# Eight token groups instead of seven, and one more sequence in head-by-head layout, in a retention and snake-FFN kernel

## The chip, the cores and the metric

The kernel runs on one core of a Trainium2 chip. The metric is the device time of one execution in microseconds (us). One core has five engines that run at the same time, each with its own instruction stream in a fixed order: TensorE (PE, matrix multiplies; its weight loads are listed as PEld), VectorE (DVE), ScalarE (ACT), GpSimd (POOL) and SyncE (SP, which here only starts transfers). Transfers (DMAs) are started from SP, ACT or POOL and run beside the engines. Matrix products land in PSUM, eight banks of 2 KB on each of 128 partitions; everything else is kept in SBUF.

## What is computed

The first part is a retention layer with a state of its own for each batch entry and head, the second a feed-forward layer with a snake activation:

```python
batch, n_heads, seq, head_dim = (4, 8, 768, 64)
gamma = 1.0 - 2.0 ** (-5.0 - np.arange(H))
for t in range(S):
    state = gamma[None, :, None, None] * state + einsum('bhd,bhe->bhde', k[:, :, t], v[:, :, t])
    y[:, :, t] = scale * einsum('bhd,bhde->bhe', q[:, :, t], state)
# y as [3072 tokens, 512]
h = x @ w_in            # 512 -> 2048
s = np.sin(alpha * h)
g = h + s * s / (alpha + 1e-09)
out = g @ w_out         # 2048 -> 512
```

## The kernel before

**Chunks and sequences.** A sequence is one batch entry: 768 tokens, cut into six chunks of 128. There are 24 chunks. The list `order` (called `P` further down) puts the four first chunks of the four sequences at the front (`e0` to `e3`, `P[0]` to `P[3]`), then the other five of each sequence: `P[4..8]` are of sequence 0, `P[9..13]` of sequence 1, `P[14..18]` of sequence 2 and `P[19..23]` of sequence 3.

**Groups and phases.** The feed-forward layer works on groups of chunks, `sizes` of them (L49). `phase(g, ...)` (L543) walks over the 16 blocks of the hidden dimension of group g. One step of it (a slot) takes one block of 128 hidden units for a group of four chunks (512 columns), or two blocks for a group of two chunks (twice 256 columns). In a slot come the first product `ph` (L425), the sine on ScalarE (L428), the square (L433, or L435 on VectorE for a few slots), a piece of attention if the table `att` has one for this slot, the sum into `gT` on VectorE (L440), and some of the second product `po` (L450) of the group before, spread evenly over the slots. A finished `po` tile is copied by ScalarE (L462) and stored by SP (L463). Group 0 and the start are written out by hand.

**Attention of a chunk.** Within a chunk, attention is a masked product of q and k, plus a product of q with the state that the sequence has so far. It has two forms. In the narrow form q, k and v of a chunk lie as 128 tokens by 8 heads: `stage_A` makes the scores (L265), VectorE masks them (L269, 128x1024), `stage_M` multiplies with the state (L299) and with v (L303), makes the new state (`stage_S`, L279), scales the result into `xT` (L310), and ScalarE copies the state (`keep_S`, L286). In the wide form (`wide(j)`, L86) the partitions hold 64 tokens twice, the lower half for heads 0 to 3 and the upper half for heads 4 to 7, so that TensorE can work as four tiles of 64x64: `scores` (L337, L341), the mask (L346, 128x768), and `burst`, which does `inter` of the old chunk (L327), `scores` of the next, and `mix` of the old one (L354, L357, L366). What `burst` leaves behind is handed to the next slot: `exit` (two VectorE products into `xT`, L377), `keep` (two VectorE sums into the float32 state `s_f`, L384 or L386) and `hand` (two copies of `s_f` into the bf16 state `s_bd`, L391, by ScalarE or GpSimd). The next `inter` of the same sequence reads `s_bd`.

**Loads.** GpSimd starts all loads of q, k and v, because they turn float32 into bf16 on the way. `load_chunk` (L83) brings one chunk of one tensor in one transfer, 128 KB in bf16. `load_seq` (L103) brings the wide chunks of a whole sequence, one tensor at a time, in eight transfers, one for each head, and is in the order q, k, v. v has to be scaled by a decay before it is used (`scale_v`, L137), for nearly all chunks on GpSimd and in the same instruction stream as the loads. That stream is written out by hand from L670 to L694; an instruction in it that waits holds up all behind it.

**Turned copies.** `turn(j)` (L256) starts a DMA on SP that writes the transposed q and k of one chunk to `qkT`; it needs all of q and k of this chunk, which for a wide chunk means all eight transfers of each. It is placed two chunks ahead: the slot that makes the scores of `P[n]` starts the turn of `P[n+2]`. SP's queue holds these turns and the stores, in order.

**Slots.** `where[n]` is the (phase, slot) at which the scores of `P[n]` and the rest of the attention of `P[n-1]` stand. Before, `where` is (1,1), (1,3), (1,6) for n = 6 to 8, then slots 0, 2, 4, 6 of phase 2 for `P[9]` to `P[12]`, and slots 2, 6, 10, 14 of phases 3 to 5. Phase g makes the attention of group g + 1. Below, (2,1) stands for slot 1 of phase 2.

Of the kernel before, what the change touches and what calls it, by code (L numbers as in the profile page):

```python
# [9 lines left out]
BF16 = mybir.dt.bfloat16  # L10
# [5 lines left out]
def kernel(  # L16
# [15 lines left out]
    nc = tc.nc  # L32
    B, H, S, D = q.shape
    C = 128
    NCH = S // C
    NJ = B * NCH
# [9 lines left out]

    order = [b * NCH for b in range(B)]
    order += [b * NCH + c for b in range(B) for c in range(1, NCH)]
    sizes = [4, 2, 2, 4, 4, 4, 4]  # L49
    assert sum(sizes) == NJ  # L50
    NG = len(sizes)
    groups = [order[sum(sizes[:g]):sum(sizes[:g + 1])] for g in range(NG)]
# [14 lines left out]
    raw = {}  # L67
# [5 lines left out]
    def load_chunk(j, names="qkv"):  # L73
        for name, src in (("q", q), ("k", k), ("v", v)):
            if name not in names:
                continue
            if name == "v":
                t = big.tile([128, H, D], BF16, name="vr", tag="vr", bufs=NJ - 9)
            else:
                if ("qk", j) not in raw:  # L80
                    raw["qk", j] = big.tile([128, 2, H, D], BF16, name="qkr", tag="qkr", bufs=NJ - 10)
                t = raw["qk", j][:, "qk".index(name)]
            nc.gpsimd.dma_start(out=t, in_=chunk_of(src, j))  # L83
            raw[name, j] = t

    def wide(j):  # L86
        return j >= 2 * NCH + 2 and j != 3 * NCH

    def load_seq(bt, names="qkv"):

# [42 lines left out]
    def scale_v(j, eng):  # L133
        t, by = raw["v", j], kg
        if wide(j):
            t, by = t.rearrange("i f p d -> i (f p) d"), kgq
        eng.tensor_mul(t, t, by[:, j % NCH, :, None].to_broadcast([128, H, D]))  # L137
# [150 lines left out]
    def stage_M(j):  # L288
        c = j % NCH
        g, i = place[j]  # L290
        if g not in xT:
            xT[g] = work.tile([128, KS, sizes[g] * C], BF16, name="xT", tag="xT", bufs=3)
        qkT, aT, vs = st["qkT", j], st["aT", j], raw["v", j]
        py = psum.tile([128, NP, 128], F32, name="py", tag="ty")
        if c > 0:
            for p in range(NP):
                for e in range(2):
                    r = slice(64 * e, 64 * e + 64)
                    nc.tensor.matmul(py[r, p, :], s_bd[c % 2][:, p, r], qkT[:, p, :],  # L299
                                     start=(p == 0), stop=True, skip_group_check=True)  # L300
        for p in range(NP):
            for e in range(2):
                nc.tensor.matmul(py[64 * e:64 * e + 64, p, :], vs[:, 2 * p + e, :], aT[:, e, p, :],  # L303
                                 start=(c == 0 and p == 0), stop=True, skip_group_check=True)
        x = xT[g][:, :, i * C:(i + 1) * C]
        if c == 0:
            nc.scalar.copy(x, py)
            return
        ps = stage_S(j) if c < NCH - 1 else None
        nc.vector.tensor_mul(x, py, qg[:, c])  # L310
        if ps is not None:
            keep_S(j, ps)
# [36 lines left out]
    def mix(j, first=None):  # L349

        py, aT, vs, c = st["py", j], st["aT", j], raw["v", j], j % NCH
        for m in range(2):
            for b, e in tiles4:
                nc.tensor.matmul(py[b][half(e), m * 128:(m + 1) * 128], vs[half(b), 0, 2 * m + e, :],  # L354
                                 aT[half(b), e, m, 0:128], start=False, stop=True, skip_group_check=True)
            for b, e in tiles4:
                nc.tensor.matmul(py[b][half(e), m * 128 + 64:(m + 1) * 128], vs[half(b), 1, 2 * m + e, :],  # L357
                                 aT[half(b), e, m, 128:192], start=False, stop=True, skip_group_check=True)
        now = j if c < NCH - 1 else first
        if now is not None:  # L360
            ks, vs = raw["k", now], raw["v", now]
            for f in range(2 if wide(now) else 1):
                for m in range(2):
                    for b, e in tiles4:
                        h = 4 * b + 2 * m + e
                        nc.tensor.matmul(py[b][half(e), 256 + 64 * m:320 + 64 * m],  # L366
                                         ks[half(b), f, 2 * m + e, :] if wide(now) else ks[:, h, :],
                                         vs[half(b), f, 2 * m + e, :] if wide(now) else vs[:, h, :],
                                         start=False, stop=True, skip_group_check=True)
        g, i = place[j]  # L370
        if g not in xT:
            xT[g] = work.tile([128, KS, sizes[g] * C], BF16, name="xT", tag="xT", bufs=3)
        x = xT[g][:, :, i * C:(i + 1) * C]

        def leave():
            for b in range(2):
                nc.vector.tensor_mul(x[:, 2 * b:2 * b + 2, :], py[b][:, 0:256].rearrange("p (m t) -> p m t", m=2),  # L377
                                     qg[:, c, 2 * b:2 * b + 2])

        def keep():  # L380
            for b in range(2):
                o, new = s_f[:, 2 * b:2 * b + 2], py[b][:, 256:384].rearrange("p (m d) -> p m d", m=2)
                if wide(now):
                    nc.vector.tensor_add(o, o, new)  # L384
                else:
                    nc.vector.tensor_copy(o, new)  # L386

        def hand():
            for e in range(2):
                copy = nc.scalar.copy if now // NCH == 2 else nc.gpsimd.tensor_copy  # L390
                copy(s_bd[(now % NCH + 1) % 2][half(e), :, half(e)], s_f[half(e)])  # L391

        more = {"exit": leave}
        if now is not None:
            more.update(keep=keep, hand=hand)
        return more
# [6 lines left out]
    def run(more, *kinds):  # L403
        for kind in kinds:
            if more and kind in more:
                more.pop(kind)()
# [136 lines left out]
    def phase(g, outs, att, nf=1, on_vector=()):  # L543


        no, done = len(outs), 0
        for n in range(FF // nf):
            more, fresh = rest[0], {}
            now = Slot(g, n * nf, nf=nf).sq("D" if n in on_vector else "A")
            run(more, "keep", "exit", "hand")  # L550
            for fn in att.get(n, ()):
                fresh.update(fn() or {})
            run(fresh, "mask")
            if fresh:
                rest[0] = fresh
            now.add()
            while done < no * (n + 1) * nf // FF:
                outs[done]()
                done += 1
# [13 lines left out]
    def SK(j):  # L573
        return lambda: keep_S(j, stage_S(j))
# [3 lines left out]
    P = order  # L578
# [91 lines left out]
    load_chunk(P[7])  # L670
    load_chunk(P[8])
    scale_v(P[6], nc.gpsimd)
    load_chunk(P[9])
    scale_v(P[7], nc.gpsimd)
    scale_v(P[8], nc.gpsimd)
    scale_v(e1, nc.gpsimd)
    load_chunk(P[10])
    for n in range(11, 15):
        scale_v(P[n - 2], nc.gpsimd)
        load_chunk(P[n])  # L680
    load_seq(2, "q")
    scale_v(P[13], nc.gpsimd)
    scale_v(e2, nc.gpsimd)
    load_seq(2, "k")
    scale_v(P[14], nc.gpsimd)
    load_seq(2, "v")
    scale_v(e3, nc.gpsimd)
    load_seq(3, "q")
    scale_v(P[15], nc.gpsimd)
    scale_v(P[16], nc.gpsimd)  # L690
    load_seq(3, "k")
    scale_v(P[17], nc.gpsimd)
    scale_v(P[18], nc.gpsimd)
    load_seq(3, "v")  # L694

    fill(1)
# [5 lines left out]
    fill(4)  # L702
    stage_M(P[5])
    fill(4)
    where = {6: (1, 1), 7: (1, 3), 8: (1, 6)}
    for g in range(2, NG - 1):
        first = P.index(groups[g + 1][0])
        for i, n in enumerate((0, 2, 4, 6) if sizes[g] == 2 else (2, 6, 10, 14)):
            where[first + i + 1] = (g, n)
    atts = {g: {} for g in range(1, NG)}  # L710

    def at(place, fn):
        atts[place[0]].setdefault(place[1], []).append(fn)

    def M_last(j):

        stage_M(j)
        nc.vector.tensor_copy(s_f, st["ps"])

    def B(old, new, first):  # L720
# [3 lines left out]
    for n in range(6, NJ + 1):  # L724
        new = P[n] if n < NJ else None
        first = new - 1 if n < NJ and new % NCH == 1 else None
        if n > 6 and wide(P[n - 1]):
            at(where[n], B(P[n - 1], new, first))
        else:
            at(where[n], lambda j=new: (scores if wide(j) else stage_A)(j))  # L730
            if n > 6:
                at(where[n], lambda j=P[n - 1], last=wide(new): (M_last if last else stage_M)(j))
            if first is not None:
                at(where[n], SK(first))
        if n + 2 < NJ:
            at(where[n], X(P[n + 2]))
        if n >= 19 and n < NJ:
            at(where[n], lambda j=new: scale_v(j, nc.gpsimd))
# [35 lines left out]
```

## Time and profile before

| what | us |
|---|---|
| three runs | 215.71, 215.79, 216.97 |
| median | 215.79 |
| the profiled execution, its own time | 216.11 |
| its span, first to last instruction | 214.3 |
| VectorE busy | 133.9 (62%) |
| ScalarE busy | 157.3 (73%) |
| GpSimd busy | 103.7 (48%) |
| TensorE's granted clock, mean | 1.000 |

The profiled execution stands 1.8 us above its span and 0.32 us above the median. TensorE is busy nearly all the time; the transfers are dense up to about 128 us and thin after that, since all of q, k and v has been loaded by then. A busy TensorE is not TensorE at its peak: the 128x512 products of L425 and L450 are shown with 379 and 380 ns each, but in a row of them they follow each other every 0.216 us (four in 0.86 us).

| line, operation | shape | count | mean ns |
|---|---|---|---|
| L428 ACT sine | 128x512 | 72 | 686 |
| L428 ACT sine | 128x256 | 32 | 470 |
| L433 ACT square | 128x512 | 82 | 630 |
| L440 DVE into gT | 128x512 | 72 | 746 |
| L440 DVE into gT | 128x256 | 32 | 476 |
| L269 DVE narrow mask | 128x1024 | 11 | 1218 |
| L346 DVE wide mask | 128x768 | 9 | 954 |
| L310 DVE narrow xT | 128x512 | 11 | 684 |
| L377 DVE wide xT | 128x256 | 18 | 416 |
| L391 ACT hand | 64x256 | 6 | 394 |

### The profile page before, as it was taken

Reading aid. Unit: us, or ns where it says so; the run is one execution under the profiler, and the core shown is the slowest. Engines: PE = TensorE matmul, PEld = TensorE weight load, DVE = VectorE, ACT = ScalarE, POOL = GpSimd, SP = SyncE. Lnnn points to the kernel's source line nnn. Section 1 sums busy time; section 2 is a strip of 40 time slices with the busy share of each in tenths; the row PEclk is TensorE's granted clock in tenths of the full one; section 3 lists DMA queues with packets and bytes.
Section 4 is the critical chain, followed back from the end, with each engine's and each line's share of the span. In section 5 each row is a group of like instructions: output and inputs, shape, how many; then the busy total and the mean of one; then the engine's idle time right before and its main releaser. Section 6 shows DMA issues by size and latency. Waiting matters only on the chain.

```text
span 214.3 us, 4656 instructions
## 1 busy us (share of the span) xinstructions
PE 201.1 (94%) x1822; PEld 108.7 (51%) x1849; DVE 133.9 (62%) x253; ACT 157.3 (73%) x299; POOL 103.7 (48%) x136
## 2 busy tenths in 40 slices
PE   7798999899999999997999999999999999999994
PEld 2444554467767664534454554554554444444453
DVE  5887859857997766866946746665765544444000
ACT  7779696757897779787697796677677778887121
POOL 8974433999397697999999213203301000000000
PEclk9999999999999999999999999999999999999999
DMA  9999999999999999999999982141011011100212
GB/s 134 146 191 185 206 207 171 154 133 240 144 159 157 136 189 155 131 97 193 161 158 115 158 133 66 35 98 54 3 50 49 3 49 49 49 38 14 98 49 98
DMA packets 101189, 24.95 MB, mean 116 GB/s; under 512 B 93728, under 2 KB 98224, under 8 KB 101168
## 3 DMA queue, kind: packets, MB, share of 16 engines
q0 software_dynamic: 77360, 13.38, 86.3%
q1 hardware_dynamic: 23664, 11.22, 26.5%
q8 instruction: 14, 0.23, 0.5%
q10 hardware_dynamic: 144, 0.07, 0.1%
q14 instruction: 7, 0.06, 0.1%
HBM read 27.27 MB, written 6.29 MB: 157 GB/s over the span
## 4 chain that ended last, share of the span: by engine, by line
PE 79%; DVE 8%; ACT 6%; DMA 3%; issue 3%; DVEq 0%; ACTq 0%
PE po L450 33%; PE ph L425 32%; ACT s L428 3%; DMA qkT<-qk_seq 3%; DVE gT L440 3%; PE spare L492 3%; ACT s L433 2%; DVE aT L269 2%; PE pa L265 2%; PE poh L473 2%; PE py L299 2%; PE py L303 1%; PE pa L337 1%; PE py L327 1%; PE ps L279 1%
## 5 line engine op out<-in xcount | busy, mean ns | idle before, releaser
L440 DVE SCALAR_TENSOR_TENSOR gT<-s,rec_alpha,ph 128x512 bf16<-128x512 f32 (+3 forms) x120 | 74.2, 638 | 55.1 <-ACT s L433 54.6
L425 PE MATMUL ph<-xT,w_in 128*128 128x512 bf16 (+3 forms) x478 | 97.9, 337 | 1.1 <-DVE xT L377 0.3
L450 PE MATMUL po<-w_out,gT 128*128 128x512 bf16 x344 | 90.8, 380 | 3.5 <-issue 2.8
L428 ACT ACTIVATE s<-ph,alpha_sb 128x512 f32<-128x512 f32 (+3 forms) x120 | 69.5, 600 | 32.9 <-PE ph L425 32.6
L425 PEld LDWEIGHTS <-w_in 128*128 128x128 bf16 x480 | 45.5, 98 | 43.0 <-issue 2.5
L433 ACT ACTIVATE s<-s 128x512 f32<-128x512 f32 (+1 forms) x90 | 55.8, 621 | 2.5
L450 PEld LDWEIGHTS <-gT 128*128 128x128 bf16 x368 | 34.0, 98 | 37.0 <-issue 0.6
L462 ACT COPY o_sb<-po 128x512 f32<-128x512 f32 x23 | 13.1, 575 | 8.5 <-PE po L450 8.4
L391 POOL CAST s_bd<-s_f 64x256 bf16<-64x256 f32 x10 | 3.9, 394 | 26.3 <-DVE s_f L384 23.2
L137 POOL TENSOR_TENSOR vr<-vr,kg 128x512 bf16<-128x512 bf16 x12 | 13.0, 1097 | 7.3 <-DMA vr<-in_v_dram 7.3
L83 POOL DMA_DIRECT2D vr<-in_v_dram x15 | 13.7, 916 | 3.5 <-DMA w_in<-in_moe_w_in_dram 1.7
L83 POOL DMA_DIRECT2D qkr<-in_q_dram x14 | 12.9, 918 | 3.6 <-DMA w_in<-in_moe_w_in_dram 1.7
L83 POOL DMA_DIRECT2D qkr<-in_k_dram x14 | 12.6, 897 | 4.0 <-DMA w_out<-in_moe_w_out_dram 3.3
L269 DVE TENSOR_TENSOR aT<-pa,mask 128x1024 bf16<-128x1024 f32 x11 | 13.4, 1218 | 0.5 <-PE pa L265 0.5
L137 POOL TENSOR_TENSOR v_seq<-v_seq,kgq 128x512 bf16<-128x512 bf16 x9 | 9.3, 1055 | 7.7 <-DMA v_seq<-in_v_dram 7.3
L103 POOL DMA_DIRECT2D qk_seq<-in_q_dram x16 | 11.3, 750 | 1.8 <-DMA vr<-in_v_dram 1.2
L103 POOL DMA_DIRECT2D qk_seq<-in_k_dram x16 | 11.2, 729 | 0.3 <-DMA qk_seq<-in_q_dram 0.3
L103 POOL DMA_DIRECT2D v_seq<-in_v_dram x16 | 11.3, 758 | 0.0
L286 ACT CAST s_bd<-ps 64x256 bf16<-64x256 f32 x24 | 8.7, 360 | 3.0 <-PE ps L279 2.7
L492 PE MATMUL spare<-warm 128*128 128x512 bf16 x27 | 8.9, 450 | 1.3 <-DVE warm L156 1.2
L310 DVE TENSOR_TENSOR xT<-py,qg 128x512 bf16<-128x512 f32 x11 | 7.5, 684 | 2.3 <-PE py L303 2.3
L346 DVE TENSOR_TENSOR aTw<-pa,maskq 128x768 bf16<-128x768 f32 x9 | 8.6, 954 | 0.5
(92 smaller groups left out, 143.9 us busy)
## 6 DMA issues: line engine op xcount, KB each, us to landing
out_dram<-o_sb SPq DMA_DIRECT2D x23, 256.0 KB, 2.3
w_in<-in_moe_w_in_dram POOLq DMA_DIRECT2D x4, 512.0 KB, 11.0
w_out<-in_moe_w_out_dram POOLq DMA_DIRECT2D x4, 512.0 KB, 14.8
vr<-in_v_dram POOLq DMA_DIRECT2D x15, 128.0 KB, 6.7
qkr<-in_q_dram POOLq DMA_DIRECT2D x14, 128.0 KB, 6.8
qkr<-in_k_dram POOLq DMA_DIRECT2D x14, 128.0 KB, 6.5
qk_seq<-in_q_dram POOLq DMA_DIRECT2D x8, 80.0 KB, 7.5
qk_seq<-in_k_dram POOLq DMA_DIRECT2D x8, 80.0 KB, 4.4
```

Source lines behind the costliest of these rows:

```text
L83: nc.gpsimd.dma_start(out=t, in_=chunk_of(src, j))
L103: nc.gpsimd.dma_start(out=o, in_=src[bt, h, cs[0] * C:, :].rearrange("(f i) d -> i f d", i=64))
L137: eng.tensor_mul(t, t, by[:, j % NCH, :, None].to_broadcast([128, H, D]))
L269: nc.vector.tensor_mul(aT.rearrange("p e n t -> p (e n) t"), pa.rearrange("p e n t -> p (e n) t"), m)
L286: nc.scalar.copy(s_bd[(j % NCH + 1) % 2][r, :, r], ps[r, :, :])
L425: nc.tensor.matmul(self.ph[:, m, :], w_in[:, i, f * 128:(f + 1) * 128], xT[g][:, i, self.lo:self.hi], start=(m == 0 and i == 0), stop=(i = ...
L428: nc.scalar.activation(out=self.s[:, m, :], in_=self.ph[:, m, :], func=ACTF.Sin, scale=alpha_sb[:, f:f + 1])
L433: nc.scalar.activation(out=self.s, in_=self.s, func=ACTF.Square)
L440: nc.vector.scalar_tensor_tensor(gT[self.g][:, f, self.lo:self.hi], self.s[:, m, :], rec_alpha[:, f:f + 1], self.ph[:, m, :], op0=ALU.mult ...
L450: nc.tensor.matmul(po[g, ts], gT[g][:, f, ts * C:(ts + 1) * C], w_out[:, f, :], start=(f == 0), stop=(f == FF - 1))
L462: nc.scalar.copy(o_sb, po[g, ts])
L492: nc.tensor.matmul(spare["ps"], warm[:, :128], warm, start=True, stop=True)
```

## The change

Groups become 4, 2, 2, 2, 2, 4, 4, 4. All chunks of sequences 1, 2 and 3 but their first ones become wide, so that six more chunks (`P[9]` to `P[14]`) are. Sequence 1 is loaded by `load_seq` in place of fifteen `load_chunk` transfers, and the eight transfers for each tensor of sequence 2 bring ten blocks of 64 tokens instead of eight. The scaling of v moves along. The order in a slot becomes `exit`, `keep`, `hand`; `hand` is ScalarE's for sequences 1 and 2. The step from narrow to wide, with its copy into `s_f`, now falls between sequences 0 and 1, at `where[9]`. Before, the table of the groups of two had slots 0, 2, 4, 6; now a group of two that is followed by another has slots 1 and 5.

```diff
-    sizes = [4, 2, 2, 4, 4, 4, 4]
+    sizes = [4, 2, 2, 2, 2, 4, 4, 4]
...
     def wide(j):
-        return j >= 2 * NCH + 2 and j != 3 * NCH
+        return j >= NCH and j % NCH > 0
...
-                copy = nc.scalar.copy if now // NCH == 2 else nc.gpsimd.tensor_copy
+                copy = nc.gpsimd.tensor_copy if now // NCH == 3 else nc.scalar.copy
...
-            run(more, "keep", "exit", "hand")
+            run(more, "exit", "keep", "hand")
...
     load_chunk(P[7])
     load_chunk(P[8])
     scale_v(P[6], nc.gpsimd)
-    load_chunk(P[9])
+    load_seq(1, "q")
     scale_v(P[7], nc.gpsimd)
+    load_seq(1, "k")
     scale_v(P[8], nc.gpsimd)
     scale_v(e1, nc.gpsimd)
-    load_chunk(P[10])
-    for n in range(11, 15):
-        scale_v(P[n - 2], nc.gpsimd)
-        load_chunk(P[n])
+    load_seq(1, "v")
+    scale_v(e2, nc.gpsimd)
     load_seq(2, "q")
-    scale_v(P[13], nc.gpsimd)
-    scale_v(e2, nc.gpsimd)
+    for j in P[9:12]:
+        scale_v(j, nc.gpsimd)
     load_seq(2, "k")
-    scale_v(P[14], nc.gpsimd)
+    for j in P[12:14]:
+        scale_v(j, nc.gpsimd)
     load_seq(2, "v")
...
-    where = {6: (1, 1), 7: (1, 3), 8: (1, 6)}
+    where = {6: (1, 1), 7: (1, 3), 8: (1, 5)}
     for g in range(2, NG - 1):
         first = P.index(groups[g + 1][0])
-        for i, n in enumerate((0, 2, 4, 6) if sizes[g] == 2 else (2, 6, 10, 14)):
+        slots = (2, 6, 10, 14) if sizes[g] == 4 else (0, 2, 4, 6) if sizes[g + 1] == 4 else (1, 5)
+        for i, n in enumerate(slots):
             where[first + i + 1] = (g, n)
...
-    def M_last(j):
-
-        stage_M(j)
+    def into_sum():
         nc.vector.tensor_copy(s_f, st["ps"])
...
-                at(where[n], lambda j=P[n - 1], last=wide(new): (M_last if last else stage_M)(j))
+                at(where[n], lambda j=P[n - 1]: stage_M(j))
             if first is not None:
                 at(where[n], SK(first))
+                at(where[n], into_sum)
```

With this, `where` is (1,5) for `P[8]`, (2,1) and (2,5) for `P[9]` and `P[10]`, (3,1) and (3,5) for `P[11]` and `P[12]`, (4,0), (4,2), (4,4), (4,6) for `P[13]` to `P[16]`, and slots 2, 6, 10, 14 of phases 5 and 6 for the rest.

## The prediction

> **What bounds the kernel now.** I read the page first, then the chain of waits in order of time, then busy time by stage, then GpSimd's timeline and the transfers' times to landing.
>
> ```profile
> span 214.3 us, 4656 instructions
> PE 201.1 (94%) x1822; PEld 108.7 (51%) x1849; DVE 133.9 (62%) x253; ACT 157.3 (73%) x299; POOL 103.7 (48%) x136
> PE 79%; DVE 8%; ACT 6%; DMA 3%; issue 3%; DVEq 0%; ACTq 0%
> ```
>
> TensorE carries the chain; one transfer holds 3% of it. The stages are phases 1 to 4, their borders the first `ph` product of each (columns: length, then busy time and instructions of each engine, clock, DMA share, GB/s).
>
> ```profile
> 47.50:61.50 14.00, 13.27 (x158) 10.00 (x160) 11.68 (x21) 11.44 (x27) 10.66 (x12) 1.00 2.07 176
> 61.50:79.96 18.46, 18.00 (x220) 12.57 (x224) 14.27 (x26) 14.94 (x35) 14.87 (x19) 1.00 1.92 163
> 79.96:107.11 27.15, 25.07 (x250) 12.61 (x252) 20.00 (x31) 22.17 (x39) 25.38 (x35) 1.00 1.75 148
> 107.11:138.57 31.46, 30.82 (x325) 15.71 (x329) 19.67 (x37) 24.67 (x42) 15.22 (x22) 1.00 1.14 113
> ```
>
> Phases 2 and 4 are full; phase 3 has 2.1 us of idle TensorE, and GpSimd works 25.38 of its 27.15. The chain says what the largest wait is, and GpSimd's timeline why:
>
> ```profile
> 91.72 5.83 DMA qkT<-qk_seq
> 97.55 0.04 issue
> 97.59 0.25 PE pa L337 x4
> ...
> 106.33 0.40 DVE s_f L384 x2
> 106.73 0.35 DVE xT L377
> 107.07 0.04 issue
> 107.11 1.02 PE ph L425 x4
> ```
>
> ```profile
> 84.19 5.48 POOL L103 DMA_DIRECT2D qk_seq<-in_k_dram  x8
> 89.60 1.13 POOL L137 TENSOR_TENSOR vr<-vr,kg 128x512 bf16<-128x512 bf16 x1
> 90.59 5.50 POOL L103 DMA_DIRECT2D v_seq<-in_v_dram  x8
> ...
> 113.39 5.75 POOL L103 DMA_DIRECT2D v_seq<-in_v_dram  x8
> ```
>
> GpSimd ends the issue of sequence 2's k at 89.67, the last of it lands at 91.5, only then can the first wide chunk be turned, and TensorE waits until 97.59. A sequence loaded head by head is late as a whole. After phase 4 the kernel does nothing but multiply.
>
> **What goes.** An attention piece on TensorE is priced by cadence. Four slots of phase 4 take 7.84 us (`po` after one burst at 112.57, after the next at 120.41), of which 4 x 1.726 = 6.90 are feed-forward: 0.94 a wide chunk. Two slots of phase 2 take 4.60 (narrow scores start at 62.47 and 67.07, at 71.78 and 76.38), of which 3.45 are feed-forward: 1.15 a narrow one. Six chunks turn wide: -1.2 us. Feed-forward itself does not change: eight products of 256 columns take 0.87, four of 512 take 0.86, and the `po` work over the phases is the same. Phase 3 is 16 x 1.294 = 20.7 plus attention of about 4.4 = 25.1, so it loses 2.0; its parts are the turn (1.1), `xT` late at the next border (0.4, mended by `exit` first) and ScalarE's lag. These 2.0 go from here. In phase 1 `stage_M(P[7])` comes a slot earlier, so the 0.26 that phase 2's first product waits for L310 goes.
>
> **What comes: ScalarE and VectorE.** Phase 5 now is the group of four after a group of two. A slot there is 1.29 on TensorE against 0.69 + 0.63 = 1.32 on ScalarE; I put 0.4 of phase 3's loss back (0 to 0.8). Phase 4 is eight slots of twice 256 columns with a burst in every second. ScalarE needs 8 x (0.84 + 0.63) + 4 x 0.80 + 2 x 0.57 = 16.1 us of some 17.6, VectorE per two slots 2 x 0.87 + 0.95 + 0.75 + 0.48 = 3.9 of 4.4: both fit, but the hand-over is tight. From the end of a slot's `ph`, the mask runs to 1.8, the sums into `gT` to 2.7, `exit` to 3.4, `keep` to 3.9, ScalarE's two copies to 4.7; the next `inter` is due at 0.94 + 0.86 + 0.87 + 0.86 + 0.87 = 4.4. That is 0.35 late, three times, 1.0 us (0 to 1.5); behind the waiting `inter` stand all products of TensorE. In phases 2, 3, 5 and 6 bursts are four slots apart, so hand-over and the moved `exit` cost nothing there: the cover is two whole slots.
>
> **What comes: sequence 1 as a whole.** `P[9]` needs all ten blocks of q and k, sixteen transfers. GpSimd's stream up to L673 is unchanged: it has scaled `P[6]` by 45.47. From there eight transfers of 80 KB take 5.75 (row 113.39), a scaling 1.02. q ends at 51.2, `scale_v(P[7])` at 52.2, k at 58.0. The last k transfer, issued at 57.3, lands 2.6 (sequence 2) to 4.0 (sequence 3) later, 59.9 to 61.3. The loads now issued at 45.47 to 47.27 took 7.6 to 9.9 to land, as the turn of `P[8]` and three stores run in 44.6 to 56.9, so 1 us more is possible; I take 61.3. The turn then takes between 3.1 (alone, the one at 132.35) and 8.1 (beside loads, the one at 48.80); I take 5.8 of the nearest case, that of 91.72, which also starts when k lands and v is being issued: `qkT` of `P[9]` at 67.1 (63.0 to 69). TensorE gets to (2,1) at 61.51 - 0.26 + 1.73 + 0.87 = 63.85. Its wait there is **3.3 us** (0 to 4.9), and nothing covers it: `stage_M(P[8])`, the state and `po` stand behind it. SP's queue has the turns of `P[9]` and `P[10]` ahead of a store, which delays only that store.
>
> GpSimd sets a second date. After k come two scalings (60.1), v (65.8), e2 (66.8), sequence 2's q (72.6), and only then `P[9]`'s v is scaled, 73.6 (up to 75.5 if issues wait for landings, as at 81.51 for 1.2 us and at 108.57 for 0.3). Without any wait TensorE is at `mix(P[9])` in (2,5) at 63.85 + 1.05 + 0.86 + 3 x 1.73 + 0.87 + 0.65 = 72.5. So this alone costs 1.1 to 3.0, and with 3.3 lost at (2,1) it is hidden; the two don't add. All later pieces have slack: `P[14]`, turned from (3,5) at about 91, needs sequence 2's k, whose issue ends at 82 to 84.
>
> Loading by heads costs GpSimd more: a chunk's 1024 pieces (128 tokens by 8 heads) take 0.87 us to issue, a head's 640 take 0.72, 30% more for the same data; the sums above hold this. The Trainium skill, "DMA: Bandwidth & Descriptors", section "Rules for kernel authors", says that two transfers to disjoint partition halves only serialize on the same engines, so nothing is won or lost in moving the data; by that rule alone, at a chunk's pace of issue, k would end 2.8 earlier and the wait be 0.5, and the trace's issue rows speak against taking it so.
>
> **Sum.** -1.2 - 2.0 - 0.26 + 0.4 + 1.0 + 3.3 = +1.2 us on the profiled execution's 216.11 (span 214.3 and 1.8 around it), 217.3; it stands 0.32 above the median of 215.79, so 217.0 for a median.
>
> **Rivals.** *Loads in time.* The turn runs as fast as alone (3.1) and k lands at 59.9 to 61: wait at (2,1) nil, only GpSimd's 1.1 at `mix`, hand-over 0.3. Then -3.46 + 1.1 + 0.3 + 0.3 = -1.8: 214.0, to 213.3 with neither of the small losses. Against it: of the 14 turns that ran beside loads none took under 4.9 us to land, and v is issued right after k. It decides if `P[9]` is turned by 64.
>
> *TensorE's clock drops in the wait.* The page's clock row is full throughout, yet the first nine fillers after the idle start take 3.69 us, 0.41 each, where later ones follow each other at 0.22: 1.75 us lost after a long idle. No later idle of TensorE exceeds 1.2 us, so nothing here shows whether 3.3 is long enough. If it is, +1.75 on the forecast: 218.8, and with the turn at 69, 220.5. It decides at a wait somewhere between 1.2 and the start's idle. The skill's "TensorE: Matmul & The Clock Gate", section "Part 1: The HAM clock gate", puts it at one free-running window of about 3.4 us, which makes our wait a borderline case.
>
> *Hand-over in phase 4.* If ScalarE's lag adds up over the four bursts (16.1 of 17.6 us), each `inter` after the first waits 1 us and phase 5 starts with full buffers: +2 on the forecast, 219. For it, ScalarE's share of 91%; against it, phase 1's 82% with no such wait.
>
> That the change doesn't act is excluded: the built kernel's order has 24 transfers of sequence 1 and fifteen wide bursts.
>
> **Chances.** Forecast (wait of 2 to 4.7, clock full) 0.52, its own range 215.4 to 218.5; in time 0.20; clock 0.21; hand-over 0.07. The range to 0.8 is 213.7 to 220.3. 1% (2.2 us) is about what a measurement can tell from no change: below 213.6 lies a good half of "in time" and a little of the forecast's edge, 0.14; above 218.0 the two slow rivals, most of them, and 0.12 of the forecast's, 0.38; between, 0.48.
>
> **What would show it.** A wait of TensorE on `qkT<-qk_seq` of some 3 us just before the first L337, near 64 to 67; if it is under 1 us, the landing of k or the turn was mis-sized. Then a wait at L354 for `v_seq` in (2,5) should appear instead. Phase 4 (twice 256 columns, burst in every second slot) should take 18.6, with L327 waiting for ScalarE's L391. Fillers' pace: `ph` products of 256 columns after the wait at 0.22 each instead of 0.108 would be the clock. No turn should delay TensorE after (2,1). I am wrong at the root if the phases before 61 us change, or if TensorE waits for loads later than phase 2.

## The result, and the profile after

The changed kernel takes 223.58 us (median of four runs, 222.49 to 225.52) against 216.18 for the kernel before in the same series: a ratio of 1.035 [1.027, 1.043]. It is slower, and above the predicted range. Executions over 1.5% longer than the fastest one of their kernel are left out of the times and ratios below. The profiled execution took 224.11, its span is 222.3, 8.0 longer than before.

The page of the changed kernel: span, TensorE's row, and the engines' shares of the chain that ended last.

```profile
span 222.3 us, 5042 instructions
PE 202.7 (91%) x1998; PEld 115.4 (52%) x2025; DVE 137.9 (62%) x287; ACT 160.5 (72%) x315; POOL 105.8 (48%) x142
PE 51%; DMA 23%; DVE 7%; ACT 7%; POOL 7%; issue 3%; POOLq 0%; SPq 0%; DVEq 0%
```

TensorE's busy time hardly grew (1.6 us), its share of the chain fell from 79% to 51%, and transfers hold 23% where they held 3%, since the chain now runs back through the loads to the start of the kernel (`w_out` 7% and `w_in` 5% among them). These shares are therefore no measure of what was lost. Where the time lies is told by stage. Phases 2 to 5 of the changed kernel do the work of phases 2 to 4 before (columns: length, then busy time and instructions of PE, PEld, DVE, ACT and POOL, granted clock, DMA share, GB/s):

```profile
62.51:84.17 21.66, 17.19 (x188) 11.57 (x188) 11.50 (x26) 13.78 (x31) 21.22 (x29) 0.92 1.71 154
84.17:100.13 15.96, 15.64 (x200) 10.93 (x200) 10.64 (x27) 13.65 (x31) 15.96 (x22) 1.00 1.68 132
100.13:120.13 20.00, 17.71 (x293) 12.33 (x296) 14.77 (x37) 15.36 (x34) 15.17 (x20) 1.00 2.22 161
120.13:146.63 26.50, 24.40 (x294) 12.54 (x296) 19.60 (x38) 22.55 (x39) 3.38 (x4) 1.00 0.48 70
```

Together 84.12 us; the three phases before took 18.51 + 27.10 + 31.45 = 77.06, with the borders at the first `ph` of each phase. That is 7.1 of the 8.0. About 1.0 more lies ahead of the change: phase 1 began at 48.63 instead of 47.50. That part of the code is the same, and over all executions of this study it began anywhere from 47.50 to 48.68, so it is scatter. Everything from phase 6 on takes the same time as before.

Three phases have idle time: phase 2 has 4.5 us and the only clock below 1.00, phase 4 has 2.3, phase 5 has 2.1. Phase 3, the same form as phase 2 with two wide bursts, has only 0.3. A part of this, 0.16 us in most slots with a burst, is listed as `issue`, in the kernel before too; the waits with a named cause are 3.98, 1.76 and 1.32 us.

**Phase 2.** The chain of waits of the changed kernel, in order of time (start, length, what):

```profile
49.39 9.12 DMA qk_seq<-in_q_dram
58.51 0.28 issue
58.79 1.40 POOL qk_seq L103 x2
60.19 3.76 DMA qk_seq<-in_k_dram
...
64.08 5.22 DMA qkT<-qk_seq
69.30 0.04 issue
69.34 0.25 PE pa L337 x4
...
70.81 1.49 PE po L450 x3
72.30 1.56 PE ph L425 x8
```

Read upwards from the first wide product at 69.34: it waited for the turned copy, that for the last transfer of k (landed at 63.95), and the issue of that one for the landing of a transfer of *q* at 58.51. TensorE stood for 3.98 us (65.36 to 69.34). Behind it its products are slow: three `po` take 1.49 where they take 0.81 behind the next burst, eight `ph` 1.56 instead of 0.87; from 73.86 the pace is the usual one. The granted clock of the same kernel says so too (columns: length, PE's busy time and instructions, clock, DMA share, GB/s):

```profile
66.74:70.16 3.42, 0.82 (x36) 1.00 1.73 158
70.16:73.57 3.41, 3.08 (x23) 0.50 1.81 212
```

It is 1.00 all through the wait, falls 0.8 us after the wait has ended, and is 1.00 again from 73.57.

GpSimd's timeline of the same kernel shows the part that was not foreseen (start, length, engine, line, operation, and in brackets idle time ahead of it and its releaser):

```profile
54.82 2.13 POOL L103 DMA_DIRECT2D qk_seq<-in_k_dram  x3 [1.39 <-DMA qk_seq<-in_q_dram]
57.34 0.72 POOL L103 DMA_DIRECT2D qk_seq<-in_k_dram  x1 [0.39 <-DMA qk_seq<-in_q_dram]
58.79 2.13 POOL L103 DMA_DIRECT2D qk_seq<-in_k_dram  x3 [0.73 <-DMA qk_seq<-in_q_dram]
```

The eight transfers of q landed at 52.38, 54.15, 54.42, 55.52, 57.06, 58.51, 59.03 and 59.63. Transfer n of k was never issued before transfer n of q, eight back, had landed. The trace's record of each of these instructions names the cause: a transfer that GpSimd starts waits for one of eight semaphores (106 to 113, in turn) and raises the same one on landing. So the wait is in the program as it was built. The issue of k thus ends at 60.92 instead of 58.0, by 2.5 us of such waits.

**Phase 4.** The chain again, a part of one turn of its loop:

```profile
104.74 0.63 ACT s L433
105.36 0.37 ACT s_bd L391
105.73 0.01 issue
105.75 0.41 ACT s_bd L391
106.16 0.05 issue
106.20 0.40 PE py L327 x4
```

The two copies of the state stand behind sine (0.85, from 103.87) and square of the slot in ScalarE's stream. The next `inter` (L327) waits for them 0.64 us here, and 0.56 in each of the next two turns. Two slots take 5.2 us where their products need 4.4.

### The profile page after: what moved, and what is told of

Same layout as the page of the kernel before. It is cut to its first block, busy times and chain, and to the rows that moved or that the text cites. A ratio compares the mean times of both kernels' runs of the same rounds, so it can differ in the third digit from the quotient of the medians.

```text
span 222.3 us, 5042 instructions
## 1 busy us (share of the span) xinstructions
PE 202.7 (91%) x1998; PEld 115.4 (52%) x2025; DVE 137.9 (62%) x287; ACT 160.5 (72%) x315; POOL 105.8 (48%) x142
## 4 chain that ended last, share of the span: by engine, by line
PE 51%; DMA 23%; DVE 7%; ACT 7%; POOL 7%; issue 3%; POOLq 0%; SPq 0%; DVEq 0%
PE po L450 24%; PE ph L425 20%; DMA w_out<-in_moe_w_out_dram 7%; DMA w_in<-in_moe_w_in_dram 5%; DMA qk_seq<-in_q_dram 4%; DVE gT L440 3%; DMA vr<-in_v_dram 3%; ACT s L428 3%; DMA qkT<-qk_seq 2%; POOL qk_seq L103 2%; POOL qkr L83 2%; ACT s_bd L391 2%; ACT s L433 2%; DMA qk_seq<-in_k_dram 2%; PE poh L473 2%
## 5 line engine op out<-in xcount | busy, mean ns | idle before, releaser
L440 DVE SCALAR_TENSOR_TENSOR gT<-s,rec_alpha,ph 128x256 bf16<-128x256 f32 (+3 forms) x136 | 76.0, 587 | 53.8 <-ACT s L433 53.3
L425 PE MATMUL ph<-xT,w_in 128*128 128x256 bf16 (+3 forms) x542 | 98.8, 318 | 2.1 <-DVE gT L440 1.6
L428 ACT ACTIVATE s<-ph,alpha_sb 128x256 f32<-128x256 f32 (+3 forms) x136 | 71.7, 559 | 32.7 <-PE ph L425 32.0
L425 PEld LDWEIGHTS <-w_in 128*128 128x128 bf16 x544 | 52.1, 98 | 42.3 <-issue 4.4
L462 ACT COPY o_sb<-po 128x512 f32<-128x512 f32 x23 | 13.1, 575 | 8.5 <-PE po L450 8.4
L137 POOL TENSOR_TENSOR v_seq<-v_seq,kgq 128x512 bf16<-128x512 bf16 x15 | 15.7, 1101 | 7.2 <-DMA v_seq<-in_v_dram 6.9
L103 POOL DMA_DIRECT2D qk_seq<-in_k_dram x24 | 17.3, 767 | 2.5 <-DMA qk_seq<-in_q_dram 2.5
L103 POOL DMA_DIRECT2D v_seq<-in_v_dram x24 | 17.4, 770 | 1.5 <-DMA qk_seq<-in_k_dram 1.5
L103 POOL DMA_DIRECT2D qk_seq<-in_q_dram x24 | 17.4, 787 | 0.4 <-DMA v_seq<-in_v_dram 0.4
L346 DVE TENSOR_TENSOR aTw<-pa,maskq 128x768 bf16<-128x768 f32 x15 | 14.3, 953 | 2.3 <-PE pa L341 1.9
L377 DVE TENSOR_TENSOR xT<-py,qg 128x256 bf16<-128x256 f32 x30 | 11.2, 415 | 0.0
L337 PE MATMUL pa<-qkT 64*64 64x128 bf16 x120 | 5.1, 230 | 4.0 <-DMA qkT<-qk_seq 4.0
```

The source lines that it names most:

```text
L103: nc.gpsimd.dma_start(out=o, in_=src[bt, h, cs[0] * C:, :].rearrange("(f i) d -> i f d", i=64))
L346: return {"mask": lambda: nc.vector.tensor_mul(aT, pa[:, :, 0:384].rearrange("p e (m t) -> p e m t", m=2), maskq[:, None, None, :].to_broa ...
L425: nc.tensor.matmul(self.ph[:, m, :], w_in[:, i, f * 128:(f + 1) * 128], xT[g][:, i, self.lo:self.hi], start=(m == 0 and i == 0), stop=(i = ...
L428: nc.scalar.activation(out=self.s[:, m, :], in_=self.ph[:, m, :], func=ACTF.Sin, scale=alpha_sb[:, f:f + 1])
L440: nc.vector.scalar_tensor_tensor(gT[self.g][:, f, self.lo:self.hi], self.s[:, m, :], rec_alpha[:, f:f + 1], self.ph[:, m, :], op0=ALU.mult ...
L462: nc.scalar.copy(o_sb, po[g, ts])
```

## The experiments

Each kernel is the changed one with the edit shown, unless it says otherwise. Lengths of phases run from one phase's first `ph` to the next one's; those of the changed kernel are 13.88, 21.66, 15.96, 20.01, 26.49, 31.03 for phases 1 to 6.

**1. The pieces of phase 2 later.**

```diff
-        slots = ... else (0, 2, 4, 6) if sizes[g + 1] == 4 else (1, 5)
+        slots = ... else (0, 2, 4, 6) if sizes[g + 1] == 4 else (4, 6) if g == 2 else (1, 5)
```

> Only the two pieces of attention in phase 2 move, from slots 1 and 5 to slots 4 and 6; loads, groups and work are as after the change. If the loss of phase 2 (21.7 us of some 15.9 us of work) is the wait for sequence 1's q and k and what follows from it, TensorE gets to the first wide scores at about 70, after the turned copy has landed (69.3): the 4 us wait for qkT goes, and the slow 1.5 us behind it. In its place a wait of about 1 us for the scaled v in slot 6, since GpSimd is done with it at 76.8. Phase 2 some 17 us, time 219 (218 to 220.5). Rival: what holds phase 2 is the transfers' rate as a whole, and the wait comes back at the next pieces; then the time stays at 222 to 224.

219.58 us, ratio 1.016 [1.011, 1.021]. The wait for the turn is gone, the clock is 1.00 and phase 2 takes 17.17, 4.5 less. What is left of the delay is the second date of GpSimd's: the wait now stands at the next burst's `mix`, as TensorE's timeline of this kernel shows.

```profile
76.20 0.25 PE L354 MATMUL py<-aTw,v_seq 64*64 64x128 bf16 x4 [0.92 <-POOL v_seq L137]
```

Phases 4 and 5 stay at 20.02 and 26.50: their losses have nothing to do with the loads.

**2. Products that keep TensorE busy in the wait.** Ahead of the first wide scores, fifteen 128x512 products into the scores' own PSUM tile, whose result is overwritten.

```diff
     def scores(j):
...
+            if j == P[9]:
+                for _ in range(15):
+                    nc.tensor.matmul(pa[:, 0, :], warm[:, :128], warm, start=True, stop=True)
```

> Fifteen 128x512 filler products (3.2 us at full clock) are put on TensorE ahead of the first wide scores, into the scores' own PSUM tile, which the scores overwrite. Data arrive as before. If TensorE's clock fell because it idled for 4 us, the granted clock of phase 2 goes from 0.92 to 1.00, the four po and eight ph products behind the wait run at 0.216 and 0.108 each again, and 1.5 us are won: 222.0 (221.3 to 222.8) against 223.6. Rival: the slow products are something else (a bank or a port held by the late loads); then the clock and the time stay, 223 to 224.5.

222.16 us, 1.029 [1.024, 1.034]. In TensorE's timeline of this kernel (lines from L335 on are three higher here) the products behind the wait have their usual pace:

```profile
64.88 3.40 PE L337 MATMUL pa<-warm 128*128 128x512 bf16 x14
...
69.20 0.82 PE L453 MATMUL po<-w_out,gT 128*128 128x512 bf16 x3
70.07 1.04 PE L428 MATMUL ph<-xT,w_in 128*128 128x256 bf16 x8
```

Three `po` and eight `ph` take 0.82 and 1.04; in the same view of the changed kernel it was 1.49 and 1.77. The granted clock is 1.000 in all four runs of it. In the four of the changed kernel it is 0.992, 0.985, 0.992 and 0.999, with times of 224.11, 225.52, 223.05 and 222.49: the one whose clock held is the one that comes near this kernel. One stretch of 3.41 us at half clock makes a mean of 0.992, two make 0.985, as the traces of the changed kernel and of experiment 5 have them. So the clock's drop is a cost of its own, about 1.1 to 1.5 us (3.41 us at half clock can cost 1.7 at most), and the wait is what brings it.

**3. Phase 4's hand-over ahead of the sine.**

```diff
         for n in range(FF // nf):
...
+            if g == 4:
+                run(more, "exit", "keep", "hand")
             now = Slot(g, n * nf, nf=nf).sq("D" if n in on_vector else "A")
```

> In phase 4 alone, exit, keep and hand of the burst before are issued ahead of the slot's sine, not behind its square. If phase 4's waits for s_bd (0.64, 0.56 and 0.56 shown, 0.8 each from the end of ph) come from the two copies standing behind sine and square on ScalarE, the copies start when s_f is ready (105.3, 109.8, 115.5 in the run after the change), and the next inter at most 0.5 late: phase 4 19 us or less in place of 20, time 222.3 (221.5 to 222.8). Rival: VectorE's exit and keep set it, or the later sine now holds up the products; then phase 4 stays within 0.4 of 20 and the time at 223.2 to 224.5.

A miss: 228.71 us, 1.057 [1.051, 1.063], slower still. TensorE's waits of this kernel in phase 4 and the start of phase 5 (us in total, times, longest):

```profile
PE py L327 <- ACT s_bd L391: 3.4, 3, 1.5
PE ph L425 <- ACT o_sb L462: 2.1, 1, 2.1
```

The copies now hold up the sine: the chain goes sum, `exit`, `keep`, copies (0.80), sine, square, sum, mask, sum, and from the second turn on takes longer (some 6.1 us) than the one it replaced. Phase 4 takes 22.75.

**4. The groups alone.** The kernel before, with the new group sizes and slots; loads, wide chunks and the order in a slot as before.

```diff
-    sizes = [4, 2, 2, 4, 4, 4, 4]
+    sizes = [4, 2, 2, 2, 2, 4, 4, 4]
...
+        slots = (2, 6, 10, 14) if sizes[g] == 4 else (0, 2, 4, 6) if sizes[g + 1] == 4 else (1, 5)
```

> The kernel before with the groups and the slot table of the change and nothing else: loads, wide chunks and the order keep, exit, hand are those of before. If the loss sits in the loads of sequence 1 and in the wide hand-over of phase 4, this one has neither: no wait on a turned copy above 0.5 us, phase 2 and 3 some 16 us each, phase 4 18 to 18.5, phase 5 26 (as phase 3 before without its wait), time 215 to 217. Rival: smaller groups themselves cost, by 16 more sines and 32 more sums into gT of 256 columns; then 218 to 220 and no single wait over 1 us.

217.26 us, 1.006 [1.002, 1.010]. Its phases 4 and 5:

```profile
94.94:113.11 18.17, 17.75 (x250) 12.57 (x253) 13.93 (x29) 14.37 (x33) 18.17 (x25) 1.00 1.90 145
113.11:139.99 26.88, 24.40 (x294) 12.55 (x296) 20.93 (x40) 23.16 (x41) 8.20 (x13) 1.00 1.02 106
```

With 16.14 and 16.15 for phases 2 and 3 the four sum to 77.34, only 0.28 above the three phases before. This kernel is the ledger for the rest: the full change differs from it by +5.52 in phase 2 (4.0 of wait, 1.5 of clock), -0.19 in phase 3, +1.84 in phase 4 and -0.39 in phase 5. Phase 1 takes 14.74 here, 0.96 of it a wait for `xT` (L310).

**5. The hand-over between sine and square.**

```diff
-            now = Slot(g, n * nf, nf=nf).sq("D" if n in on_vector else "A")
+            now = Slot(g, n * nf, nf=nf)
+            if g == 4:
+                run(more, "exit", "keep", "hand")
+            now.sq("D" if n in on_vector else "A")
```

> In phase 4 alone, the hand-over's two copies stand on ScalarE between the slot's sine and its square, not behind the square (ahead of the sine they made it worse). If phase 4's slots follow a loop (inter, rest of burst, po, ph, sine 0.84, square 0.63, copies 0.80, next inter: 5.14 us for two slots whose products take 4.4), taking the 0.63 out of it gives some 4.5 for two slots, VectorE's keep allowing: phase 4 18.6 to 19.2 us in place of 20, time 222.3 (221.3 to 223.2) with the clock's scatter. Rival: the loop closes over VectorE as it did with the copies ahead of the sine (square late, gT late, mask late); then phase 4 stays at 20 or more, time 223.5 or more.

224.54 us, 1.036 [1.031, 1.041], a miss for the theory that ScalarE's order costs the time: L327 waits 0.64, 0.43 and 0.77, and phase 4 takes 20.09. The time saved ahead of the copies is lost behind them: phase 5 takes 26.90, 0.4 more.

**6. The loads alone.** The changed kernel with the seven groups of before.

```diff
-    sizes = [4, 2, 2, 2, 2, 4, 4, 4]
+    sizes = [4, 2, 2, 4, 4, 4, 4]
```

> The changed kernel with the seven groups of before, so that only loads, wide chunks and order of the hand-over are changed. The first wide scores are due in slot 0 of phase 2, at about 63, with the turned copy landing at 68 to 69: a wait of 5 to 6 us for qkT, clock lost behind it (1 to 2 us), then about 2 us for the scaled v in slot 2, and the tight hand-over in phase 2's three later bursts (0.7 each). 223 to 227, phase 2 some 28 us. Rival: the loss is of the eight groups and not of the loads; then the time is below 219.

229.46 us, 1.058 [1.052, 1.064], above the expected span. TensorE waits 7.42 us for the first turned copy (to 70.92) instead of 3.98, and phase 3 takes 29.45. With the seven groups, phase 2 has its first piece in slot 0 and makes four pieces in eight slots. The new groups, which cost little alone, pay back nearly half of what the late loads cost: they ask for `P[9]` later and for two chunks a phase, not four.

**7. Three mends at once:** edit 1, edit 5, and the scaling of `e2` moved behind that of `P[9]` to `P[11]` in GpSimd's stream.

```diff
-    scale_v(e2, nc.gpsimd)
     load_seq(2, "q")
     for j in P[9:12]:
         scale_v(j, nc.gpsimd)
+    scale_v(e2, nc.gpsimd)
```

> The changed kernel with three mends: phase 2's pieces in slots 4 and 6, the scaling of e2's v behind that of P[9] to P[11], and the copies between sine and square in phase 4. If waits for loads, clock and hand-over are what the change lost, phase 2 takes 16.2, no L354 wait for v_seq is left, phase 4 19: 217.2 (216.2 to 218.5). What is left over 215.7 is then phase 5, 26 us of 24.5. Rival: time stays with 219.6, what is taken off in one phase coming back in the next.

A miss: 219.54 and 221.24 us, 1.016 [1.007, 1.026]. Phase 2 takes 17.02 with 0.78 of waiting for `v_seq`, phases 4 and 5 take 20.09 and 26.89. The moved scaling gains 0.15 over the first experiment, and edit 5 gains nothing here either.

**8. The same without squares on VectorE** in phase 5.

```diff
-              (4, 12) if sizes[g] > sizes[g - 1] else ())
+              ())
```

> As the run before it, and in phase 5 no square is VectorE's (slots 4 and 12 before): ScalarE then has 16 sines and squares. If phase 5's waits of TensorE for gT (0.34 and 0.98) come from VectorE falling behind where exit, keep and a square meet, phase 5 takes 25.0 to 25.6 in place of 26.1 and the time is 0.5 to 1.0 under the run before it. Rival: ScalarE (1.32 us a slot against 1.29) is the bound there; then phase 5 is 26.2 or more and the time the same or up to 1 higher.

220.61 us, 1.017 [1.010, 1.023]. Phase 5 goes from 26.89 to 27.36: two squares more for ScalarE make it 0.47 longer.

**9. The state out of phase 4's loop.** The copies go to a spare tile, and `inter` of `P[13]` to `P[15]` reads zeros; the state is so left out of three chunks, with every instruction still there.

```diff
-        qkT, s = st["qkT", j], s_bd[j % NCH % 2]
+        qkT, s = st["qkT", j], s_zero if j in P[13:16] else s_bd[j % NCH % 2]
...
+                to = s_off if P[12] <= now < P[15] else s_bd[(now % NCH + 1) % 2]
```

> The changed kernel with the hand-over cut in phase 4: ScalarE makes the same two copies of s_f at the same place, but into a spare tile, and inter of P[13], P[14] and P[15] reads a tile of zeros, so that the state is left out of these three chunks' output. Every engine has the instructions that it had. If phase 4's 20.0 us are the loop from one burst's state to the next, inter waits for nothing and phase 4 takes 17.8 to 18.3; the time falls by about 2 against the run after the change with the same clock. Rival: ScalarE or VectorE is simply full in slots of twice 256 columns with a burst in every second; then phase 4 stays above 19.

One execution, 223.05 us. Phase 4 by stage:

```profile
100.75:118.97 18.22, 17.62 (x293) 12.52 (x296) 13.99 (x35) 15.61 (x34) 16.28 (x21) 1.00 1.97 158
```

1.8 less, with 15.6 us of work on ScalarE as before and no wait at L327. The engines can carry this phase; the loop through the state cannot be walked every second slot.

**10. The kernel before, mended.** `exit` ahead of `keep`, and the phase 3 piece that waits for the turn one slot later.

```diff
-            run(more, "keep", "exit", "hand")
+            run(more, "exit", "keep", "hand")
...
-        ... else (2, 6, 10, 14)):
+        ... else (2, 6, 11, 14) if g == 3 else (2, 6, 10, 14)):
```

> The kernel before with two small edits that the runs point to: exit ahead of keep, and in phase 3 the piece with the first wide scores in slot 11 in place of 10. If a sequence loaded as a whole is only late, by about 1.1 us at 97.6, the wait for qkT is gone and so is the 0.3 for xT at the border to phase 4: phase 3 takes 25.7 to 26.2 in place of 27.1, time 1.0 to 1.4 below before (ratio 0.994 to 0.995). Rival: phase 3's length is ScalarE's, and the wait was hidden in it: phase 3 26.8 or more, ratio 0.998 to 1.002.

216.04 against 216.12 us (medians), ratio 0.997 [0.993, 1.001]: no difference that can be told. Phase 3 falls from 27.10 to 26.72. The wait for the turn (0.9) is gone, and a wait of 0.8 for `v_seq` at L354 stands in its place.

**11. The pieces spread out.**

```diff
+    for n, s in enumerate(((2, 4), (2, 6), (3, 1), (3, 4), (3, 7), (4, 2), (4, 4), (4, 6))):
+        where[9 + n] = s
```

> The changed kernel with the pieces of phases 2 to 4 at other slots: (2,4), (2,6), (3,1), (3,4), (3,7), (4,2), (4,4), (4,6), so that no data are waited for in phase 2 and two pairs of bursts in place of three stand two slots apart. If the hand-over costs 0.8 for each such pair and nothing else in phase 4 is late, phases 3 and 4 together take 35.5 in place of 36.3 and the time is 218.5 to 219.3. Rival: small slots are full on ScalarE or VectorE whatever the order; then phases 3 and 4 take 36.2 or more and the time is that of the later slots, 219.6.

219.40 us, 1.012 [1.004, 1.019]. Phases 3 and 4 take 16.73 + 18.34 = 35.1 instead of 36.0: two tight pairs of bursts instead of three, and two waits of 0.6 at L327 instead of three. One slot between two bursts costs 0.6 each time; two slots cost nothing.

**12. Four squares on VectorE in phase 5,** on top of edit 1.

```diff
-              (4, 12) if sizes[g] > sizes[g - 1] else ())
+              (0, 4, 8, 12) if sizes[g] > sizes[g - 1] else ())
```

> The kernel with its second-phase pieces in slots 4 and 6 (219.61, phase 5 26.50 us, no load waits in it), and in phase 5 (a group of four after a group of two) four squares on VectorE, in slots 0, 4, 8 and 12, where two were. Phase 5's products fill 24.40 of its 26.50 us; the other 2.1 is what is asked for. Without any square on VectorE it took 27.36 against 26.89 (another variant). If ScalarE alone sets the phase, it gives up 2 x 0.63 us there, half of which I expect at TensorE: phase 5 falls to 25.3 to 26.0 and the kernel to some 219.0. If VectorE's chain of sum, mask and exit sets it (the releaser of both waits is the sum into gT), two more squares of 0.70 there make it longer: 26.8 to 27.9. No change (26.4 to 26.6) would mean that the waits come from the order at the phase's border, not from either engine's load. All other phases as in the kernel it is built on: 17.2, 16.3, 20.0 and 31.0.

218.5 us, 1.011 [1.008, 1.015]. Of this profiled execution (221.35, longer than the median by idle time ahead of phase 5 and after phase 6) only phase 5 is read:

```profile
116.59:142.62 26.03, 24.40 (x294) 12.57 (x297) 20.99 (x40) 21.42 (x37) 3.37 (x4) 1.00 0.59 80
```

26.03 instead of 26.50: shorter, as with ScalarE as the bound, by a little less than the 0.5 to 1.2 expected of it. No variant with sequence 1 loaded by heads beats the kernel before.

## Why the prediction was wrong

It missed the profiled execution by 6.8 us (217.3 against 224.11). Of this, 1.3 lies ahead of phase 2, which began 1.0 later and not 0.26 earlier; most of that is the scatter told above. In phases 2 to 5 the terms of the sum make +1.5, and 7.1 were measured. The 5.5 between them are, with experiment 4 as the ledger, 0.7 of a longer wait, 1.5 of clock, 0.8 of hand-over, 1.5 for the groups and 1.0 for the wide chunks and the order in a slot. By the prediction's own steps:

- **The wait at (2,1), 3.3 forecast.** Right in place and cause: L337 waited 3.98 for `qkT<-qk_seq`. The turn took 5.2 (5.8 taken); the last k landed at 63.95 (61.3 taken, and 62.3 held possible). The term that was mis-sized is the end of k's issue: 58.0 supposes that GpSimd issues without waiting. The prediction knew such waits, "at 81.51 for 1.2 us", and put them into the date of v, but not into that of k. The longer wait is +0.7; that the turn was faster and TensorE came later (65.36, not 63.85) hid the rest. So the near figure for the wait is in part luck.
- **The clock rival (0.21) came true on top of the forecast.** The sum held nothing for it; this step failed too. Two groups of products that should take 1.68 us took 3.05, 1.4 lost; the ledger of experiment 4 gives 1.5. The wait of 3.3 had been called a borderline case; at 4.0 in the trace the clock fell, and it did so in three of four runs. The prediction's own line for turn and clock together, 220.5 "with the turn at 69", describes what happened in phase 2: the turn landed at 69.30. The Trainium skill's page "TensorE: Matmul & The Clock Gate", section "Part 1: The HAM clock gate", has the clock fall to half after an idle window of about 3.4 us that runs free of the program. The trace agrees with the half clock (0.50) and with the length (3.41 us), but the window need not be idle throughout: in the one ahead of the fall TensorE was busy for 0.82 us. The one run of the four that kept its clock at 0.999 has no trace, so its wait is not on record.
- **The hand-over in phase 4, 1.0 forecast (0 to 1.5).** Right in kind, mis-sized. Phase 4 was to take 18.6 and took 20.0; with the state out of the loop it takes 18.2. So the hand-over costs 1.8. The waits were 0.64, 0.56 and 0.56 where 0.35 was worked out from the chain of single operations. The rival that ScalarE is too full, each `inter` waiting 1 us, falls with experiment 9: with the same work on ScalarE and the loop open, nothing waits.
- **"These 2.0 go from here."** This step failed as well. It took phase 3's idle time of before (27.10 less 25.02 busy) apart into a turn, a late `xT` and ScalarE's lag, and let all of it go. Phase 5, the new group of four after a group of two, waits for no load at all and has the same idle: 26.50 less 24.40 is 2.1. The largest waits with a cause, of phase 3 before and of phase 5 after the change (us in total, times, longest):

```profile
PE pa L337 <- DMA qkT<-qk_seq: 0.9, 1, 0.9
...
PE ph L425 <- DVE gT L440: 1.3, 2, 1.0
```

  In both phases 0.6 more is `issue`. Before, 0.3 for `xT` and 0.2 for ScalarE's copy L462 come to the turn's 0.9; after, TensorE waits for `gT` instead. The groups alone show the same in time: without the 0.4 that `exit` was to mend, the prediction's terms for them make -1.2, and in experiment 4 phases 2 to 5 take 0.28 more. Experiment 10 can't decide it for the kernel before, since a wait of 0.8 for v took the turn's place. Squares on VectorE bear on the length: in two pairs of kernels, two squares more on ScalarE cost 0.47 (experiment 8) and two fewer gain 0.47 (experiment 12). So much of the 2.0 belongs to the form of the phase, and the 0.4 put back for it (0 to 0.8) should have been some 2.0.
- **Six wide chunks, 1.2 less.** Too much. The two bursts of phase 3 gain 0.19 over the two narrow pieces in the kernel with the groups alone, 0.1 each instead of 0.21, and phase 4 gains nothing even with the state left out (18.22 against 18.17). The 0.39 that phase 5 gains is not theirs: its chunks are wide in both kernels. There the wait of 1.0 for `xT` (L377) at its end goes, with `exit` ahead of `keep`, and 0.5 of it comes back as a longer wait for `gT`.
- **GpSimd's second date, hidden behind the first.** Right: it appears as 0.92 at L354 only when the first wait is removed, as had been said for that case. So is "no turn should delay TensorE after (2,1)", and the work after phase 5 is the same.
- **The 0.26 at phase 2's start:** this wait is gone; phase 1 took 13.88 instead of 14.01, within scatter.

The direction was left open: faster, same and slower had 0.14, 0.48 and 0.38. The sum of +1.2 was a small difference of gains read too high and losses read too low.

What stays open is what holds phase 5 beyond the squares. Four of them on VectorE leave 1.6 us of idle there. A kernel that issues sequence 1's loads earlier was not tried.

## What to carry over

Idle time with a releaser's name is not yet a gain: ask what is late next, and price a phase by another one of the same form that lacks the wait. A state that is handed from burst to burst through three engines has a loop time of its own; compare that with the distance of the bursts, not each engine's load with the phase. Where a date rests on a stream of issues, look in the trace for issues that wait for landings, and lay that rule over all of the stream.

## What the runs showed of the hardware

In this program a transfer started by GpSimd waits for the landing of the one eight back, by the eight semaphores told above, and not by anything that the runs show of the chip itself: with transfers of q that took 8.0 us (median) to land, the eight transfers of k took 8.2 us to issue (52.67 to 60.92), where eight take 5.75 without a wait.

TensorE's clock: waits of 3.9 to 7.4 us brought the mean clock of the profiled executions down to 0.985 to 0.992, in experiments 5, 6 and 9 too. But the length of a wait alone does not say whether the clock falls. In experiment 3 it held after a wait of 2.99 us, which ended at 67.76, and fell after one of only 2.10, which ended at 123.23. The granted clock of experiment 3, with TensorE's busy time (columns as in phase 2):

```profile
66.11:69.52 3.41, 1.60 (x43) 1.00 1.83 168
...
120.72:124.13 3.41, 1.31 (x7) 1.00 0.02 8
124.13:127.55 3.42, 3.42 (x31) 0.50 0.93 211
```

The clock changes only at the borders of equal stretches of 3.41 us: up to the falls in the changed kernel and in experiments 3 and 5, the traces record full clock for 64.85, 119.47 and 61.44 us, which is 19, 35 and 18 times 3.413, and the half clock lasts one or two such stretches. Where the borders lie differs from run to run (at 70.16 in the changed kernel, at 70.65 in experiment 9). What tells is how long TensorE works within one stretch. The clock fell behind those with 0.82 us (the changed kernel), 1.31, 1.45, 0.00 and 0.69 (experiments 3, 5, 6 and 9), and not behind those with 1.60 (experiment 3) and 1.69 (experiment 12). The wait of 2.99 us was divided by a border; that of 2.10 lay within one stretch. This rule is worked out from five falls; no run tried to move a wait across a border.
